# Last stage with the engines' work in an order written out by hand, and operand stores a tick apart

## The chip, the cores and the metric

The kernel runs on one core of a Trainium2 chip. A time is the device time of one execution in microseconds (us). The engines are TensorE (PE; PEld is its weight load), VectorE (DVE), ScalarE (ACT), GpSimd (POOL) and SyncE (SP), which issues the DMAs here. Each takes its instructions in the order in which the program wrote them, and waits on semaphores for the others.

## The reference

Attention, a layer of routed experts, and a rational layer are chained; only the last two matter here. With `x` of 1536 tokens by 512:

```python
def _moe_ref(x, w_gate, w1, w2):          # 8 experts, 512 -> 1024 -> 512
    P = softmax-like weights of x @ w_gate, normalised 8 times by rows and columns
    for e in range(E):
        out += P[:, e:e + 1] * (np.maximum(x @ w1[e], 0.0) @ w2[e])

def _moe2_ref(x, w_in, w_out, a, b):      # 512 -> 2048 -> 512
    h = x @ w_in
    P = a[0] + a[1] * h + a[2] * h**2 + a[3] * h**3
    Q = 1.0 + np.abs(b[0]) * np.abs(h) + np.abs(b[1]) * h**2
    return (P / (Q + 1e-06)) @ w_out
```

`w_in` and `w_out` arrive as 64-bit floats, which the kernel turns into 32-bit ones itself.

## The kernel before, in words

Every 32-bit matrix is split into a high part (rounded by a copy into the matmul type) and a low part (the difference), and a product takes three matmuls: high by high, high by low, low by high.

**Expert stage (up to about 1125 us).** It runs 30 weight slices by 2 halves of the tokens, in blocks of seven products (a Strassen-like scheme on 2 by 2 quarters, 42 matmuls of 384 columns) with the second matmuls of earlier blocks as fillers between them (`block`, lines 1014 to 1077). `sub_weights` splits the next slice's weights on GpSimd and issues its loads on SP's queue. After each product but the third, `step` calls `tick` (line 884). From the third weight slice on a tick also runs one job of the conversion of `w_in` and then `w_out` (`cvjobs`: five jobs per piece of 128 by 256: round, exponents, turn, join, add). Each time a column of `w_in` is converted, `op_jobs` (line 837) queues the preparation of its seven or eight operands in `opq`: sums of quarters on GpSimd, and `op_split` (line 831), a ScalarE cast of the high part and a GpSimd subtraction for the low part into one of two buffers (tag `t3`). `op_store` (line 826) writes a finished operand to DRAM. On each tick that is not an exponent job, `tick` first stores what was split before and then runs the next group of `opq`.

**Last stage (about 1125 us to the end).** 16 blocks: two halves of the tokens (j, 768 each) by eight column pairs of `w_in` (v, 256 columns). Two are `plain` blocks (line 1266: four groups of 12 matmuls); 14 are `seven` blocks (line 1289). A `seven` block has seven products through PSUM banks X and Y (Z shares Y's bank), each bank with one buffer: products 1, 2, 4 and 6 go to X and ScalarE copies X after each (lines 1305, 1308, 1314, 1321), products 3, 5 and 7 go to Z or Y and VectorE adds them (lines 1311, 1318, 1325). The results are `x1` (half 1, complete with the sixth product) and `x0` (half 0, complete with the seventh). `gate` (line 1218) computes the rational function of one half, 128 by 768, in five steps:
- one: three ScalarE activations (lines 1224 to 1226)
- two: three VectorE operations (1229 to 1231)
- three: logarithm and exponential on ScalarE (1234, 1235)
- four: three VectorE operations (1238 to 1240)
- five: the high part `hh` by a ScalarE cast (1245) and the low part `hl` by a GpSimd subtraction (1246)

The work tiles `ab`, `sq`, `ta` have two buffers, `hh` and `hl` four, `x0` two, `x1` one. `second` (line 1198) multiplies one tile of 128 tokens of a gated half with `w_out`: three matmuls of 512 columns, the fillers; a half has six of them, so a block brings twelve. They accumulate in six PSUM tiles for all of j.

The order was made by slots: `slot` (line 1182) runs what is due by its number, then up to two fillers that are due. There are seven slots to a block, after each product; `later` sets a step's slot, `gate(..., d, d2)` starts half 1's step one in slot 1 after its call and half 0's in slot 3, one step a slot, and its fillers 9 and 11 slots after. So a block's last slot holds five of half 0 of the block before, and then one of its own half 1, before the next block's first copy (line 1305).

The second token half's sums and splits (`x_parts` on GpSimd, `x_sums` on VectorE, `x_out` on ScalarE and VectorE) are due in slots of blocks 4 to 6.

Of the kernel before, what the change touches and what calls it, by code (L numbers as in the profile page):

```python
# [22 lines left out]
def kernel(  # L23
# [802 lines left out]
    def op_store():  # L826
        while ops:
            o, t = ops.pop()
            nc.sync.dma_start(f_ops[o:o + P, :], t.bitcast(F32).rearrange("p a t f -> p (a t f)"))

    def op_split(v_, name, x):
        t = vpool.tile([P, 2, 2, P], F32R, tag="t3", name=f"w{name}_o{v_}")
        nc.scalar.copy(t[:, 0], x)
        nc.gpsimd.tensor_sub(t[:, 1], x, t[:, 0].bitcast(F32))
        ops.append(((v_ * 8 + NAMES.index(name)) * P, t))

    def op_jobs(v_):

        q11, q12, q21, q22 = (wf[v_, k][:, :, f * P:(f + 1) * P] for f in range(2) for k in range(2))
        sp = lambda n, x: lambda: op_split(v_, n, x)  # L840
        add, sub = nc.gpsimd.tensor_add, nc.gpsimd.tensor_sub
        opq.append([sp("A22", q22)])
        if v_ < PLAIN:
            opq.append([sp("A21", q21)])
        opq.append([lambda: add(q22, q21, q22), sp("A11", q11)])
        opq.append([lambda: sub(q21, q11, q21)])
        opq.append([lambda: sub(q11, q22, q11), sp("A12", q12)])
        opq.append([lambda: sub(q12, q12, q11), sp("S1", q22)])
        opq.append([sp("S3", q21)])
        opq.append([sp("S2", q11)])  # L850
        opq.append([sp("S4", q12)])
        opq.append([])

    def cv_store():
        if not cvs:
# [28 lines left out]
    def tick(cv=False):  # L884

        point[0] += 1
        if g2q and g2q[0][0] <= point[0] or not g2q:
            run_job()
        if g2q and g2q[0][0] <= point[0]:
            g2q.pop(0)[1]()  # L890
        if cv and cvjobs:
            f = cvjobs.pop(0)
            f()
            if f is not cv_exponents and opq:
                op_store()
                for g in opq.pop(0):
                    g()

    lgs = {}

# [203 lines left out]
    def x_parts(j, ms=(11, 12, 22, 21)):  # L1104
        for m in ms:
            k, t = {11: (0, 0), 12: (0, 1), 22: (1, 1), 21: (1, 0)}[m]
            o = j * HT + t * NW
            a, b = (y[:, 2 * k:2 * k + 2, o:o + NW].bitcast(F32) for y in (xh, xl))
            nc.gpsimd.tensor_add(tf[m], a, b)
# [60 lines left out]
        load_w2(0, c)  # L1170
    n = NW
    W = 2 * n
    now = [0]
    due = {}
    fills = []
    outs = {}
    used = [0]

    def later(d, f, *args):
        due.setdefault(now[0] + d, []).append(lambda: f(*args))  # L1180

    def slot(k=2):
        for f in due.pop(now[0], []):
            f()
        now[0] += 1
        while k and fills and fills[0][0] <= now[0]:
            fills.pop(0)[1]()
            k -= 1

    def op():  # L1190
        t = got[used[0]]
# [23 lines left out]
            k = len(pairs) % (2 * NV)  # L1215
            load_w2(k // 2, 1 - k % 2)

    def gate(j, v, c, x, d, d2):

        nm = f"{j}_{v}_{c}"  # L1220
        ab, sq, ta = (buf(t, f"{t}_{nm}") for t in ("ab", "sq", "ta"))

        def one():
            nc.scalar.activation(ab, x, AF.Abs, scale=coef[:, 4:5])
            nc.scalar.activation(sq, x, AF.Square)
            nc.scalar.activation(ta, x, AF.Identity, scale=coef[:, 3:4], bias=coef[:, 2:3])

        def two():
            nc.vector.scalar_tensor_tensor(out=ab, in0=sq, scalar=coef[:, 5:6], in1=ab, op0=ALU.mult, op1=ALU.add)
            nc.vector.tensor_mul(ta, ta, x)  # L1230
            nc.vector.scalar_tensor_tensor(out=ta, in0=ta, scalar=coef[:, 1:2], in1=x, op0=ALU.add, op1=ALU.mult)

        def three():
            nc.scalar.activation(sq, ab, AF.Ln, bias=c1)
            nc.scalar.activation(sq, sq, AF.Exp, scale=-1.0)

        def four():
            nc.vector.scalar_tensor_tensor(out=ab, in0=ab, scalar=1.0 + 1e-6, in1=sq, op0=ALU.add, op1=ALU.mult)
            nc.vector.scalar_tensor_tensor(out=sq, in0=ab, scalar=2.0, in1=sq, op0=ALU.subtract, op1=ALU.mult)
            nc.vector.scalar_tensor_tensor(out=ta, in0=ta, scalar=coef[:, 0:1], in1=sq, op0=ALU.add, op1=ALU.mult)  # L1240

        def five():
            hh = hp2.tile([P, W], F32R, tag="hh", name=f"hh_{nm}")
            hl = hp2.tile([P, W], F32R, tag="hl", name=f"hl_{nm}")
            nc.scalar.copy(hh, ta)  # L1245
            nc.gpsimd.tensor_sub(hl, ta, hh.bitcast(F32))  # L1246
            ht[j, v, c] = (hh, hl)

        for i, f in enumerate((one, two, three, four, five)):
            later(d + i, f)  # L1250
        m = 2 * NV * j + 2 * v + 1 - c
        for t in range(W // P):
            fills.append((now[0] + d2, lambda t=t: second(j, v, c, t, m)))

    def three_passes(ps, w, get, start, stop, go):
        for t in range(2):
# [6 lines left out]
    def xs(k, o):  # L1263
        return lambda t: (xh[:, 2 * k + t, o:o + n], xl[:, 2 * k + t, o:o + n])

    def plain(v, j):

        for c in (1, 0):
            ws = [op() for _ in range(2)]
            x = buf(f"x{c}", f"x{c}_{j}_{v}", 2 - c)  # L1270
            for half in range(2):
                ps = psm.tile([P, 512], F32, tag="mm", name=f"p_{j}_{v}_{c}_{half}")[:, :n]
                for k in range(2):
                    for t in range(2):
                        mh, ml = xs(k, j * HT + half * n)(t)
                        a = k == t == 0
                        nc.tensor.matmul(ps, lhsT=ws[k][:, 0, t], rhs=mh, start=a, stop=False)
                        nc.tensor.matmul(ps, lhsT=ws[k][:, 0, t], rhs=ml, start=False, stop=False)
                        nc.tensor.matmul(ps, lhsT=ws[k][:, 1, t], rhs=mh, start=False, stop=k == t == 1)
                nc.scalar.copy(x[:, half * n:(half + 1) * n], ps)  # L1280
                if half:
                    gate(j, v, c, x, 1 if c else 3, 11)
                    load_op()
                    load_op()
                slot()
                if c or not half:
                    slot()

    def seven(v, j):

        o1, o2, ot = j * HT, j * HT + n, j * n
        psum = lambda t, nm: psx.tile([P, 512], F32, tag=t, name=f"{nm}_{j}_{v}")[:, :n]

        def tt(i):
            return lambda t: (th[i][:, t, ot:ot + n], tl[i][:, t, ot:ot + n])

        def product(ps, get, start):
            three_passes(ps, op(), get, start, True, {} if start else {"skip_group_check": True})

        X, Z = psum("X", "X2"), psum("Y", "Z2")  # L1300
        x0 = buf("x0", f"x0_{j}_{v}")
        x1 = buf("x1", f"x1_{j}_{v}", 1)
        s1, s2, s3 = x0[:, 0:n], x0[:, n:W], x1[:, n:W]
        product(X, xs(0, o1), True)
        nc.scalar.copy(s1, X)
        slot()
        product(X, tt(0), False)
        nc.scalar.copy(s2, X)
        slot()
        product(Z, xs(1, o1), True)  # L1310
        nc.vector.tensor_add(s1, s1, Z)
        slot()
        product(X, tt(1), False)
        nc.scalar.copy(s3, X)
        slot()
        Y = psum("Y", "Y2")
        product(Y, xs(0, o2), True)
        nc.vector.tensor_add(s3, s3, Y)
        slot()
        product(X, tt(2), False)  # L1320
        nc.scalar.copy(x1[:, 0:n], X)
        gate(j, v, 1, x1, 1, 9)
        slot()
        product(Y, xs(1, o2), False)
        nc.vector.tensor_add(s2, s2, Y)
        gate(j, v, 0, x0, 3, 11)
        slot(0)

    x_sums()
    later(1, x_out, 0, 22)  # L1330
    later(3, x_out, 0, 12)
    later(5, x_out, 0, 21)
    for i, m in enumerate((11, 12, 22, 21)):
        later(7 * 4 + 2 * i, x_parts, 1, (m,))
        later(7 * 5 + 2 + 2 * i, x_out, 1, (22, 12, 21, 11)[i])
    later(7 * 5 + 1, x_sums)
    for j in range(2):
        for v_ in range(NV):
            if j == 0 and v_ < PLAIN:
# [40 lines left out]
```

## Time and profile before

| | us |
|---|---|
| median of 3 runs | 1461.36 (1457.35 to 1464.21) |
| the profiled execution | 1462.85 |
| its span, first to last instruction | 1461.1 |
| TensorE busy, whole span | 1385.9 (95%) |
| VectorE, ScalarE, GpSimd busy | 1080.1, 544.2, 880.4 |

The page's forty slices of 36.5 us give each engine's busy share in tenths (9 is 90% or more) and TensorE's granted clock in tenths of full speed:

```profile
PE   7999999999999999999999999999999887888887
DVE  7785587777777768786777777777767788777666
ACT  6674323322222222222222222222223665565654
POOL 7644656688879879788777767777731142221122
PEclk9999999999999999999999999999999898999998
```

A wait row reads: the engine and line that stood idle, and the instruction whose end let it go on. Busy time of a matmul is modelled from its start; distances between starts are the better measure.

### The profile page before, as it was taken

How to read it: one execution, taken by the hardware profiler on the slowest of the kernel's cores; microseconds unless marked ns; L12 is line 12 of the kernel's file. 1: busy time of each engine (PE TensorE's matmuls, PEld its weight loads, DVE VectorE, ACT ScalarE, POOL GpSimd, SP SyncE). 2: the span in 40 equal slices, each digit the busy share in tenths (PEclk: the TensorE clock that was granted, in tenths of full speed). 3: DMA queues.
4: the chain of work that ended last, by engine and by line, in shares of the span. 5: the costliest groups of instructions: out<-in, count | busy, mean ns of one | idle time of the engine just before them, and what ended most of it. 6: DMA issues, size and time to landing. Idle time of an engine off the chain costs nothing.

```text
span 1461.1 us, 20671 instructions
## 1 busy us (share of the span) xinstructions
PE 1385.9 (95%) x7427; PEld 1225.3 (84%) x7427; DVE 1080.1 (74%) x1731; ACT 544.2 (37%) x1138; POOL 880.4 (60%) x1092
## 2 busy tenths in 40 slices
PE   7999999999999999999999999999999887888887
PEld 5788988988888888888888888888888776777776
DVE  7785587777777768786777777777767788777666
ACT  6674323322222222222222222222223665565654
POOL 7644656688879879788777767777731142221122
PEclk9999999999999999999999999999999898999998
DMA  9430111223222223222232222222213443454432
GB/s 260 112 99 6 44 39 64 66 87 108 73 87 102 71 88 101 78 89 94 61 91 84 69 72 73 79 68 84 74 37 94 135 150 119 151 181 145 148 95 72
DMA packets 116534, 137.03 MB, mean 94 GB/s; under 512 B 26320, under 2 KB 69328, under 8 KB 116432
## 3 DMA queue, kind: packets, MB, share of 16 engines
q1 hardware_dynamic: 116432, 135.71, 30.4%
q8 instruction: 59, 0.97, 0.3%
q14 instruction: 43, 0.35, 0.1%
HBM read 108.94 MB, written 26.74 MB: 93 GB/s over the span
## 4 chain that ended last, share of the span: by engine, by line
PE 71%; POOL 11%; DVE 7%; ACT 5%; issue 2%; DMA 2%; SPq 0%; POOLq 0%; ACTq 0%; DVEq 0%
PE p_v L185 9%; PE p_v L184 9%; PE p_v L183 9%; PE X L1032 5%; PE X L1033 5%; PE X L1034 4%; PE Y L1033 2%; PE Y L1032 2%; PE Y L1034 2%; PE o L1209 2%; PE o L1207 2%; PE o L1208 2%; PE p L183 2%; PE p L185 1%; PE p L184 1%
## 5 line engine op out<-in xcount | busy, mean ns | idle before, releaser
L1093 DVE SCALAR_TENSOR_TENSOR accs<-p_v,Pt,accs 128x512 f32<-128x512 f32 x336 | 250.1, 745 | 84.8 <-PE p_v L185 81.7
L185 PE MATMUL p_v<-w2h_v,hl_v 128*128 128x512 f32 x720 | 286.8, 398 | 0.0
L184 PE MATMUL p_v<-w2l_v,hh_v 128*128 128x512 f32 x720 | 285.2, 396 | 0.0
L183 PE MATMUL p_v<-w2h_v,hh_v 128*128 128x512 f32 x720 | 282.5, 392 | 0.0
L1246 POOL TENSOR_TENSOR hl<-ta,hh 128x768 fp32r<-128x768 f32 x32 | 68.7, 2147 | 252.5 <-ACT hh L1245 225.0
L1041 DVE SCALAR_TENSOR_TENSOR hl_v<-s,hh_v 128x384 fp32r<-128x384 f32 x180 | 126.3, 702 | 110.0 <-ACT hh_v L1040 109.6
L1040 ACT ACTIVATE hh_v<-s 128x384 fp32r<-128x384 f32 x180 | 94.7, 526 | 287.9 <-DVE s L1055 143.3
L185 PEld LDWEIGHTS p_v<-w2h_v,hl_v 128*128 128x128 f32 x720 | 135.5, 188 | 29.0
L183 PEld LDWEIGHTS p_v<-w2h_v,hh_v 128*128 128x128 f32 x720 | 135.9, 189 | 17.1
L184 PEld LDWEIGHTS p_v<-w2l_v,hh_v 128*128 128x128 f32 x720 | 135.6, 188 | 17.0
L109 POOL TENSOR_TENSOR wS<-S,wS 128x256 fp32r<-128x256 f32 x120 | 98.5, 820 | 14.4 <-ACT wS L106 4.7
L108 POOL TENSOR_SCALAR wS<-S 128x256 fp32r<-128x256 f32 x116 | 51.8, 446 | 88.1 <-PE X L1034 86.8
L1047 ACT COPY s<-X 128x384 f32<-128x384 f32 x60 | 28.7, 479 | 189.3 <-PE X L1034 189.3
L1032 PE MATMUL X<-th,wS 128*128 128x384 f32 x240 | 81.3, 339 | 8.4 <-ACT s L1052 8.2
L799 POOL TENSOR_SCALAR ce<-ce 128x256 uint32<-128x256 uint32 x64 | 71.1, 1110 | 25.4 <-DVE ce L787 25.4
L109 POOL TENSOR_TENSOR w2l_v<-sb,w2h_v 128x512 fp32r<-128x512 f32 x60 | 82.0, 1367 | 5.0
L1207 PE MATMUL o<-o2h,hh 128*128 128x512 f32 x192 | 80.7, 421 | 3.7 <-ACT hh L1245 2.7
L1209 PE MATMUL o<-o2h,hl 128*128 128x512 f32 x192 | 81.0, 422 | 3.1 <-POOL hl L1246 3.1
L1033 PE MATMUL Y<-xl,wS 128*128 128x384 f32 x240 | 81.2, 338 | 0.0
L1033 PE MATMUL X<-tl,wS 128*128 128x384 f32 x240 | 81.1, 338 | 0.0
L1034 PE MATMUL X<-th,wS 128*128 128x384 f32 x240 | 80.8, 337 | 0.0
L1208 PE MATMUL o<-o2l,hh 128*128 128x512 f32 x192 | 80.7, 421 | 0.0
(272 smaller groups left out, 3652.9 us busy)
## 6 DMA issues: line engine op xcount, KB each, us to landing
sa<-in_moe_w_dram SPq DMA_DIRECT2D x30, 512.0 KB, 3.6
sb<-in_moe_w_dram SPq DMA_DIRECT2D x30, 512.0 KB, 4.2
oS<-f_ops SPq DMA_DIRECT2D x56, 256.0 KB, 3.6
oA<-f_ops SPq DMA_DIRECT2D x50, 256.0 KB, 3.4
cv<-in_moe_w_in_dram SPq DMA_DIRECT2D x32, 256.0 KB, 3.9
f_ops<-wS_o SPq DMA_DIRECT2D x32, 256.0 KB, 2.1
cv<-in_moe_w_out_dram SPq DMA_DIRECT2D x32, 256.0 KB, 3.1
o2h<-f_out SPq DMA_DIRECT2D x32, 256.0 KB, 2.7
```

Of the source, the lines that this page charges most:

```text
L109: nc.gpsimd.tensor_sub(lo, src, hi.bitcast(F32))
L183: nc.tensor.matmul(ps, lhsT=sh, rhs=mh, start=(i == 0), stop=False)
L184: nc.tensor.matmul(ps, lhsT=sh, rhs=ml, start=False, stop=False)
L185: nc.tensor.matmul(ps, lhsT=sl, rhs=mh, start=False, stop=(i == n_k - 1))
L1032: nc.tensor.matmul(ps, lhsT=w[:, 0, t], rhs=mh, start=start and t == 0, stop=False, **go)
L1033: nc.tensor.matmul(ps, lhsT=w[:, 0, t], rhs=ml, start=False, stop=False, **go)
L1034: nc.tensor.matmul(ps, lhsT=w[:, 1, t], rhs=mh, start=False, stop=t == 1, **go)
L1041: nc.vector.scalar_tensor_tensor(out=hl, in0=src, scalar=0.0, in1=hh.bitcast(F32), op0=ALU.max, op1=ALU.subtract)
L1093: nc.vector.scalar_tensor_tensor(out=a, in0=ps, scalar=Pt[:, g, e:e + 1], in1=a, op0=ALU.mult, op1=ALU.add)
L1207: nc.tensor.matmul(ps, lhsT=hh[:, o], rhs=wh, start=first, stop=False, **go)
L1208: nc.tensor.matmul(ps, lhsT=hh[:, o], rhs=wl, start=False, stop=False, **go)
L1209: nc.tensor.matmul(ps, lhsT=hl[:, o], rhs=wh, start=False, stop=True, **go)
```

## The change

Two places. In the expert stage, `op_jobs` now queues pairs: one entry splits an operand and then runs the sums that follow it, the next entry stores it. A tick takes one entry; on an exponent job it takes one only if that is a store.

In the last stage the slots are gone. `gate` returns its steps as a list (five only casts, a new six makes the low part, for half 1 on VectorE and for half 0 on GpSimd as before), and `seven` and `plain` name at each place which steps of which earlier block run: `run(b - 1, 0, 1)` is step one of half 0 of block b-1. `fill(k)` runs up to k fillers that belong to a block at least two earlier; a `seven` block has them in groups of 4, 4, 2, 2. The first token half's `x_out` calls all stand ahead of the first plain block; the second half's sums and splits are a list `jobs2`, one entry per block, taken after the steps that follow the first copy.

```diff
+        def put(n, x, *pre):
+            opq.append(lambda: (op_split(v_, n, x), [f() for f in pre]))
+            opq.append(op_store)
+
+        put("A22", q22)
...
+        put("A11", q11, lambda: add(q22, q21, q22))
+        put("A12", q12, lambda: sub(q21, q11, q21), lambda: sub(q11, q22, q11))
+        put("S1", q22, lambda: sub(q12, q12, q11))
...
-            if f is not cv_exponents and opq:
-                op_store()
-                for g in opq.pop(0):
-                    g()
+            if opq and (f is not cv_exponents or opq[0] is op_store):
+                opq.pop(0)()
...
+    def fill(k):
+        while k and fills and fills[0][0] <= count[0]:
+            fills.pop(0)[1]()
             k -= 1
...
+        def six():
...
+            (nc.vector if c else nc.gpsimd).tensor_sub(hl, ta, hh.bitcast(F32))
...
-            fills.append((now[0] + d2, lambda t=t: second(j, v, c, t, m)))
+            fills.append((count[0] + 2, lambda t=t: second(j, v, c, t, i)))
+        return [one, two, three, four, five, six]
+    def run(b, c, *steps):
+        for i in steps:
+            if (b, c) in pipe:
+                pipe[b, c][i - 1]()
...
+        act = {0: lambda: (run(b - 2, 0, 5, 6), run(b - 1, 0, 1)),
+               1: lambda: (run(b - 1, 1, 2, 3), run(b - 1, 0, 2)),
+               2: lambda: (run(b - 1, 0, 3), run(b - 1, 1, 4, 5, 6)),
+               3: lambda: run(b - 1, 0, 4)}
...
+        run(b - 1, 1, 2)
         product(X, xs(0, o1), True)
         nc.scalar.copy(s1, X)
-        slot()
+        run(b - 2, 0, 5, 6)
+        run(b - 1, 0, 1)
+        run(b - 1, 1, 3)
+        run(b - 1, 0, 2)
+        if jobs2:
+            jobs2.pop(0)()
+        fill(4)
         product(X, tt(0), False)
         nc.scalar.copy(s2, X)
-        slot()
+        run(b - 1, 0, 3)
         product(Z, xs(1, o1), True)
         nc.vector.tensor_add(s1, s1, Z)
-        slot()
+        fill(4)
+        run(b - 1, 1, 4)
         product(X, tt(1), False)
         nc.scalar.copy(s3, X)
-        slot()
+        run(b - 1, 1, 5)
         Y = psum("Y", "Y2")
         product(Y, xs(0, o2), True)
         nc.vector.tensor_add(s3, s3, Y)
-        slot()
+        run(b - 1, 1, 6)
+        run(b - 1, 0, 4)
+        fill(2)
         product(X, tt(2), False)
         nc.scalar.copy(x1[:, 0:n], X)
-        gate(j, v, 1, x1, 1, 9)
-        slot()
+        pipe[b, 1] = gate(j, v, 1, x1)
+        run(b, 1, 1)
+        fill(2)
         product(Y, xs(1, o2), False)
         nc.vector.tensor_add(s2, s2, Y)
-        gate(j, v, 0, x0, 3, 11)
-        slot(0)
+        pipe[b, 0] = gate(j, v, 0, x0)
+        count[0] += 1
...
+    jobs2 += [lambda: None, lambda: x_parts(1, (11, 12)), lambda: x_parts(1, (22, 21)), x_sums]
+    jobs2 += [both(lambda: x_out(1, 22), lambda: x_out(1, 12)), both(lambda: x_out(1, 21), lambda: x_out(1, 11))]
```

After the last block the steps that remain run in the order two of half 1, five and six of the block before's half 0, one of half 0, three of half 1, two and three of half 0, four to six of half 1, four to six of half 0; then all 24 fillers that are left.

## Rows read from the trace of the kernel before

**Rows 1.** Windows (us; busy us and count by engine; granted clock; DMA share; GB/s).

```profile
740.00:760.00 20.00, 20.00 (x102) 18.11 (x101) 13.88 (x25) 4.64 (x10) 12.50 (x18) 1.00 0.14 41
1127.00:1461.00 334.00, 281.20 (x1251) 244.22 (x1249) 247.40 (x250) 202.09 (x276) 78.78 (x36) 0.91 0.42 133
1336.40:1356.76 20.36, 17.50 (x78) 15.33 (x78) 14.48 (x16) 11.89 (x17) 4.31 (x2) 0.92 0.44 142
510.00:520.00 10.00, 7.29 (x26) 6.24 (x25) 3.62 (x6) 2.10 (x5) 9.42 (x14) 0.70 0.50 181
670.00:680.00 10.00, 7.44 (x33) 6.42 (x32) 4.76 (x7) 2.56 (x7) 9.59 (x12) 0.89 0.50 165
```

**Rows 2.** TensorE's waits, whole span: total us, times, longest.

```profile
PE X L1258 <- ACT x L1305: 38.0, 12, 5.6
PE X L1032 <- ACT s L1052: 8.2, 4, 2.7
```

**Rows 3.** Line 1305: count, ns min/median/max, first and last start.

```profile
L1305 ACT COPY x<-X x14: 452/455/481, 1155.8 to 1417.4; 128x384 f32<-128x384 f32 x14
```

**Rows 4.** Timeline of one block, ScalarE and TensorE (start, us, instruction, idle before).

```profile
1332.74 0.83 ACT L1245 CAST hh<-ta 128x768 fp32r<-128x768 f32 x1 [3.50 <-DVE ta L1240]
...
1336.48 0.69 PE L1258 MATMUL X<-th,oS 128*128 128x384 f32 x1 [2.89 <-ACT x L1305]
...
1338.56 0.63 PE L1207 MATMUL o<-o2h,hh 128*128 128x512 f32 x1
...
1339.17 0.94 ACT L1234 ACTIVATE sq<-ab,c 128x768 f32<-128x768 f32 x1
...
1340.58 0.33 PE L1258 MATMUL Z<-xh,oA 128*128 128x384 f32 x1
...
1341.64 0.39 PE L1207 MATMUL o<-o2h,hh 128*128 128x512 f32 x1
...
1343.03 0.33 PE L1258 MATMUL X<-th,oS 128*128 128x384 f32 x1
```

**Rows 5.** Timeline, VectorE, the same block, and a split before it.

```profile
1135.58 0.95 DVE L1123 TENSOR_TENSOR tl<-accs,th 128x768 fp32r<-128x768 f32 x1
...
1335.17 1.15 DVE L1229 SCALAR_TENSOR_TENSOR ab<-sq,coef,ab 128x768 f32<-128x768 f32 x1 [2.01 <-ACT sq L1225]
...
1337.23 1.02 DVE L1231 SCALAR_TENSOR_TENSOR ta<-ta,coef,x 128x768 f32<-128x768 f32 x1
...
1341.91 0.56 DVE L1311 TENSOR_TENSOR x<-x,Z 128x384 f32<-128x384 f32 x1 [3.66 <-PE Z L1260]
...
1342.38 0.95 DVE L1238 SCALAR_TENSOR_TENSOR ab<-ab,sq 128x768 f32<-128x768 f32 x1
...
1347.22 2.49 DVE L1231 SCALAR_TENSOR_TENSOR ta<-ta,coef,x 128x768 f32<-128x768 f32 x1
```

**Rows 6.** Timeline, GpSimd beside VectorE, two places.

```profile
1189.25 5.04 POOL L1109 TENSOR_TENSOR accs<-xh,xl 128x768 f32<-128x768 f32 x2
...
1190.03 2.57 DVE L1230 TENSOR_TENSOR ta<-ta,x 128x768 f32<-128x768 f32 x1
...
1346.39 2.50 POOL L1246 TENSOR_TENSOR hl<-ta,hh 128x768 fp32r<-128x768 f32 x1 [10.88 <-ACT hh L1245]
```

**Rows 7.** Timeline, 507 to 514: GpSimd, SP's queue, ScalarE.

```profile
507.24 1.30 POOL L109 TENSOR_TENSOR w2l_v<-sb,w2h_v 128x512 fp32r<-128x512 f32 x1
...
508.56 0.38 SPq L228 DMA_DIRECT2D sb<-in_moe_w_dram  x1
...
513.77 0.41 ACT L833 CAST wS_o<-wf 128x256 fp32r<-128x256 f32 x1 [5.71 <-DMA f_ops<-wS_o]
```

**Rows 8.** Timeline: the sums at the stage's start; TensorE and GpSimd at its end.

```profile
1126.13 4.07 DVE L1113 TENSOR_TENSOR accs<-accs 128x768 f32<-128x768 f32 x4
...
1431.76 0.35 PE L1258 MATMUL Y<-xh,oS 128*128 128x384 f32 x1
...
1451.33 1.83 POOL L1246 TENSOR_TENSOR hl<-ta,hh 128x768 fp32r<-128x768 f32 x1 [4.79 <-issue]
```

More of the change, by code (lines that the diff above doesn't have):

```diff
@@ L839, in op_jobs @@
         q11, q12, q21, q22 = (wf[v_, k][:, :, f * P:(f + 1) * P] for f in range(2) for k in range(2))
-        sp = lambda n, x: lambda: op_split(v_, n, x)
         add, sub = nc.gpsimd.tensor_add, nc.gpsimd.tensor_sub
-        opq.append([sp("A22", q22)])
+        def put(n, x, *pre):
+            opq.append(lambda: (op_split(v_, n, x), [f() for f in pre]))
+            opq.append(op_store)
+        put("A22", q22)
         if v_ < PLAIN:
[L844 to L852, printed above, removed]
+            put("A21", q21)
+        put("A11", q11, lambda: add(q22, q21, q22))
+        put("A12", q12, lambda: sub(q21, q11, q21), lambda: sub(q11, q22, q11))
+        put("S1", q22, lambda: sub(q12, q12, q11))
+        put("S3", q21)
+        put("S2", q11)
+        put("S4", q12)
     def cv_store():
@@ L1172 @@
     W = 2 * n
-    now = [0]
-    due = {}
     fills = []
@@ L1177 @@
     used = [0]
[L1179 to L1186, printed above, removed]
+    def fill(k):
+        while k and fills and fills[0][0] <= count[0]:
             fills.pop(0)[1]()
             k -= 1
+    count = [0]
     def op():
@@ L1216, in second, with gate @@
             load_w2(k // 2, 1 - k % 2)
-    def gate(j, v, c, x, d, d2):
+    def gate(j, v, c, x):
         nm = f"{j}_{v}_{c}"
@@ L1243, in five @@
             hh = hp2.tile([P, W], F32R, tag="hh", name=f"hh_{nm}")
+            nc.scalar.copy(hh, ta)
+            m["hh"] = hh
+        def six():
+            hh = m["hh"]
             hl = hp2.tile([P, W], F32R, tag="hl", name=f"hl_{nm}")
-            nc.scalar.copy(hh, ta)
-            nc.gpsimd.tensor_sub(hl, ta, hh.bitcast(F32))
+            (nc.vector if c else nc.gpsimd).tensor_sub(hl, ta, hh.bitcast(F32))
             ht[j, v, c] = (hh, hl)
-        for i, f in enumerate((one, two, three, four, five)):
-            later(d + i, f)
-        m = 2 * NV * j + 2 * v + 1 - c
+        m = {}
+        i = 2 * NV * j + 2 * v + 1 - c
         for t in range(W // P):
-            fills.append((now[0] + d2, lambda t=t: second(j, v, c, t, m)))
+            fills.append((count[0] + 2, lambda t=t: second(j, v, c, t, i)))
+        return [one, two, three, four, five, six]
+    pipe = {}
+    def run(b, c, *steps):
+        for i in steps:
+            if (b, c) in pipe:
+                pipe[b, c][i - 1]()
     def three_passes(ps, w, get, start, stop, go):
@@ L1266, in plain @@
     def plain(v, j):
+        b = count[0]
+        act = {0: lambda: (run(b - 2, 0, 5, 6), run(b - 1, 0, 1)),
+               1: lambda: (run(b - 1, 1, 2, 3), run(b - 1, 0, 2)),
+               2: lambda: (run(b - 1, 0, 3), run(b - 1, 1, 4, 5, 6)),
+               3: lambda: run(b - 1, 0, 4)}
+        i = 0
         for c in (1, 0):
@@ L1280, in plain @@
                 nc.scalar.copy(x[:, half * n:(half + 1) * n], ps)
[L1281 to L1284, printed above, removed]
-                slot()
-                if c or not half:
-                    slot()
+                act[i]()
+                i += 1
+            load_op()
+            load_op()
+            if c:
+                x1 = x
+        pipe[b, 1] = gate(j, v, 1, x1)
+        pipe[b, 0] = gate(j, v, 0, x)
+        run(b, 1, 1)
+        count[0] += 1
     def seven(v, j):
+        b = count[0]
         o1, o2, ot = j * HT, j * HT + n, j * n
@@ L1318, in seven @@
         nc.vector.tensor_add(s3, s3, Y)
-        slot()
+        run(b - 1, 1, 6)
+        run(b - 1, 0, 4)
+        fill(2)
         product(X, tt(2), False)
         nc.scalar.copy(x1[:, 0:n], X)
-        gate(j, v, 1, x1, 1, 9)
-        slot()
+        pipe[b, 1] = gate(j, v, 1, x1)
+        run(b, 1, 1)
+        fill(2)
         product(Y, xs(1, o2), False)
         nc.vector.tensor_add(s2, s2, Y)
-        gate(j, v, 0, x0, 3, 11)
-        slot(0)
+        pipe[b, 0] = gate(j, v, 0, x0)
+        count[0] += 1
     x_sums()
[L1330 to L1336, printed above, removed]
+    jobs2 = []
+    for m in (22, 12, 21):
+        x_out(0, m)
+    both = lambda *fs: lambda: [f() for f in fs]
+    jobs2 += [lambda: None, lambda: x_parts(1, (11, 12)), lambda: x_parts(1, (22, 21)), x_sums]
+    jobs2 += [both(lambda: x_out(1, 22), lambda: x_out(1, 12)), both(lambda: x_out(1, 21), lambda: x_out(1, 11))]
     for j in range(2):
@@ L1346 @@
                 seven(v_, j)
-    while fills or due:
-        slot()
+    b = count[0]
+    run(b - 1, 1, 2)
+    run(b - 2, 0, 5, 6)
+    run(b - 1, 0, 1)
+    run(b - 1, 1, 3)
+    run(b - 1, 0, 2, 3)
+    run(b - 1, 1, 4, 5, 6)
+    run(b - 1, 0, 4, 5, 6)
+    count[0] += 2
+    fill(len(fills))
 _INS = ['q', 'k', 'v', 'moe_w_gate', 'moe_w1', 'moe_w2', 'moe2_w_in', 'moe2_w_out', 'moe2_a', 'moe2_b']
```

## The prediction

> **What bounds the kernel now.** I read the busy time by stretch first. In the stage with the routed experts TensorE is never idle: 20.00 of 20 us at granted clock 1.00 [rows 1]. In the last stage it is busy 281 of 334 us, at 0.91 [rows 1]. So time can be won in the last stage, and in the earlier one only where TensorE stalls. TensorE's waits name two places [rows 2]: the second product of a seven-product block (line 1258), 38.0 us in 12 waits for ScalarE's copy at line 1305, and line 1032 in the expert stage, 8.2 us in 4 waits for ScalarE's copy at line 1052.
>
> The 14 seven-product blocks start 20.12 us apart on average: line 1305 runs 14 times, first at 1155.8, last at 1417.4, and 261.6 / 13 = 20.12 [rows 3]. One such block shows why. ScalarE stands 3.50 us at the cast `hh` (line 1245), because VectorE has the last gate operation (line 1240) late; behind it in ScalarE's queue stand three gate operations and then the copy that empties X. TensorE waits 2.89 us for that copy [rows 4]. After the wait the six matmuls of the product take 2.08 us (1336.48 to 1338.56) and the two fillers behind them 2.02 us; at the higher clock a product takes 1.06 (1340.58 to 1341.64) and a pair of fillers 1.39 (1341.64 to 1343.03). So the wait brings 1.66 us at 1.2 GHz, until the clock is back at 2.4. 2.89 + 1.66 = 4.6 us of each block are not work; 7 x 1.05 + 6 x 1.39 = 15.7 us are.
>
> VectorE is not the bound: 14.48 of the block's 20.36 us [rows 1], and it stands 3.66 and 2.01 us in the same block [rows 5]. Both waits go back to the same stall: the first is for a product that TensorE starts late, the second for a gate operation behind the late cast.
>
> **The change: last stage.** The order written out puts the copy of X first in each block, right behind the first product, and the cast of half 0 after that copy. The gate of half 0 of block b-1 now runs in block b, its cast and low part in block b+1, so no cast that TensorE's next product stands behind waits for work of its own block. Four fillers (2.8 us) stand between each of the first copies and the product that needs the bank. I lay one steady block out in order, from the start of the seventh product (time 0), with durations from [rows 4 to 6]:
> - TensorE: seventh product 0, first product of the next block 1.05, four fillers 2.1, second product 4.9, third 5.9, four fillers 7.0, fourth 9.7, fifth 10.8, two fillers 11.9, sixth 13.2, two fillers 14.3, end 15.7.
> - ScalarE: copy 2.3, cast of half 0 2.7, its three gate operations 3.4 to 6.9 (cast, three operations and copy took 3.7, from 1332.74 to 1336.48; here the third overwrites `ta` and waits for GpSimd's low part), logarithm and exponential of half 1 to 8.5 (0.94 the first [rows 4], the second taken as less), second copy 8.5 to 8.9, needed at 9.7. That is 0.8 us of room. Busy 11.89 us per block before [rows 1] and as much after, so it is not the bound.
> - VectorE: sum into `x0` 1.8, three operations of half 1 from 2.3, three of half 0 from 6.6, sum 9.5, needed by TensorE at 10.8; three of half 1 9.9 to 12.9, sum 13.3, then it waits about 0.5 us for ScalarE's cast, does the new low part to 14.7, three of half 0 to 17.6.
>
> VectorE's sum decides. From line 1238 at 1342.38 to line 1231 at 1347.22 are five gate operations: 0.97 each [rows 5], so 12 take 11.6. Three sums of 0.47 (1341.91 to 1342.38) are 1.4. The low part, 128x768, comes from GpSimd: a subtraction of that form took VectorE 0.95 [rows 5]; in a row of instructions I count 0.9. GpSimd's low part of half 0 stays. When GpSimd ran one at 1346.39 (2.50 us), VectorE's line 1231, given to it at 1347.22, took 2.49 instead of 1.02 [rows 5, 6]: the two take turns, and it costs VectorE 1.5. That happens once a block now and once after (half 1 can't collide any more; half 0, which met an idle VectorE, now will). 11.6 + 1.4 + 0.9 + 1.5 = 15.4, with the wait for the cast 15.85 us. TensorE's 15.7 is just below. I take 15.85; bounds are 15.7 (TensorE alone) and 17.4 (VectorE loses two turns, + 1.5). From 20.12 that is 13 x 4.27 = 55.5 us.
>
> VectorE is then full, so work that its waits hid before now costs. The second half's sums and splits go through it once: four sums, 4.07 as at the stage's start [rows 8]; four low parts, 4 x 0.9; four sums on GpSimd, of which two took 5.04 us together and held up VectorE's line 1230 to 2.57 [rows 6]: a turn of 1.5 to 1.6 each, 3.1 per pair. 4.1 + 3.6 + 6.2 = 13.9 us; bounds 7 (half of it falls in waits) and 20 (TensorE comes back from each stall at the lower clock). Steady part: 55.5 - 13.9 = 41.6 us gained. The loads on SP's queue stay tied to the same products, nine operands and four pairs ahead; in the shorter block their 142 GB/s (share 0.44) become 182 (0.57) [rows 1], which 510 to 520 moved with ease [rows 1]. I cost them at nothing; if one came late, TensorE would wait for a load at line 1258 or 1207, which it never does now.
>
> **Start and end of the stage.** Three splits now stand ahead of the plain blocks' copies (1.7 us of VectorE, 2.2 of ScalarE), but three PSUM buffers let TensorE go on, and no fillers stand in the plain blocks, where four ran before. Laid out as above the first X copy comes near 1152 instead of 1155.8 with as many fillers done: I take 3 gained, bounds -2 and 6. At the end 24 fillers remain in either order. Before, the seventh product of the last block starts at 1431.76 and the last low part ends at 1451.33 + 1.83, that is 21.4 later [rows 8]; in the new order (two operations of half 0 beside GpSimd's turn, then four, cast, low part, four, cast, low part) I get 20.3: 1 gained, bounds -2 and 3.
>
> **The change: stores of w_in's operands.** ScalarE's first half of an operand reuses one of two buffers; it waited 5.71 us for the store of the operand before last [rows 7], because that store stood on SP's queue behind a weight load (issued 508.56) that itself waited for GpSimd's split (507.24 + 1.30) [rows 7]. Splits came a tick apart; now split and store take turns, so a buffer comes up again after five ticks instead of two or three. A tick is a sixth of a block's 78 matmuls, at 102 in 20 us [rows 1] 2.55 us, so five are 13 us. A store held up 5 us lands in time. The exponent tick now issues a store, never a split. The sums behind a split run after it on GpSimd, which nobody waits for within two ticks. What goes: 8.2 us of waits [rows 2], and the lower clock behind two: 510 to 520 has 26 matmuls and 670 to 680 has 33, where 51 fit [rows 1], so (25 + 18) x 20 / 102 = 8.4 us are lost there, against 2.71 + 2.56 of idleness. 8.2 + 3.1 = 11.3 us. Bounds 0 (the waits move elsewhere) and 13.
>
> **Sum.** 41.6 + 3 + 1 + 11.3 = 57 us. The profiled execution took 1462.85 us (span 1461.1), 1.5 above the median of the runs; against it 1406, against the median 1404. I say 1404.
>
> **Rivals.**
> *VectorE loses two turns to GpSimd per block* (17.4 us): 1404 + 13 x 1.5 = 1424. For: GpSimd's low part now runs while VectorE always has work. Against: before, a 2.50 us run cost only the one operation.
> *The stores bring nothing*, as ScalarE waits for VectorE's last conversion or GpSimd instead: 1404 + 11 = 1415. Against: the long waits name the store.
> *TensorE is the bound and the second half's work falls in gaps*: 13 x 0.15 + 7 + 5 better, 1390.
> *The clock, on the other side:* TensorE, held by a nearly full VectorE in every block, falls to 1.2 GHz again and again. Matmuls take twice as long at that clock, and VectorE's extra work then hides. It decides from 36% of TensorE's work at it: 15.7 x 1.36 = 21.3 us per block, 13 x 1.2 = 15 us lost, as much as start, end and stores gain. At half, 15.7 x 1.5 = 23.5 us per block, 13 x 3.4 = 44 lost, less 15: 1491. For: the 2.89 us wait did bring the lower clock. Against: it came back within the same block, before the third product (1340.58) [rows 4], and by my layout no stop over about 1 us is left in a steady block. The Trainium skill says in "TensorE: Matmul & The Clock Gate", section "A second HAM failure mode: psum-queue depth-cycling", that frequent short idles between groups of matmuls can make the clock swing between its levels; by that rule this rival would come true, and no row here shows such short idles bring it.
>
> **Chances.** Forecast (1394 to 1413) 0.55, two turns 0.18, stores nothing 0.08, better 0.12, clock 0.05, anything else 0.02. The range that holds the time 8 times in 10 is 1389 to 1429: it takes in both ends of the steady period. About 0.5% (7 us) is what a measurement can tell. Faster by more than that 0.94; within it 0.02; slower 0.04.
>
> **What would show it.** After: the first copies of a block some 15.9 us apart from the eighth block on, TensorE's waits for them gone, granted clock 0.97 or more in those blocks, VectorE busy over 14.9 us of each; blocks 3 to 7 about 18 to 20 us. Line 1032 without waits for ScalarE, and ScalarE's split without waits for stores. I am wrong if VectorE idles over 2 us per steady block, if TensorE's clock stays near 0.9, or if ScalarE's second copy comes later than the four fillers before it end.

## The result, and the profile after

The changed kernel takes 1403.89 us (median of 4 runs, 1403.49 to 1404.32) against 1462.35 (1457.35 to 1464.21) for the kernel before: ratio 0.9605, 95% interval 0.9581 to 0.963. The forecast was 1404. Its profiled execution took 1403.65 us, with a span of 1401.9.

The windows of the changed kernel (columns as in [rows 1]): the last stage, one steady block from first copy to first copy, two blocks with two `x_parts` each, and two stretches of the expert stage.

```profile
1112.00:1401.90 289.90, 264.62 (x1254) 230.83 (x1252) 261.44 (x266) 202.40 (x276) 43.09 (x20) 0.96 0.48 153
1327.20:1343.20 16.00, 15.93 (x79) 14.06 (x79) 15.35 (x17) 11.98 (x16) 2.09 (x1) 1.00 0.54 179
1153.74:1172.77 19.03, 15.90 (x79) 14.03 (x78) 18.38 (x17) 11.96 (x17) 7.19 (x3) 1.00 0.48 152
1172.77:1193.22 20.45, 17.33 (x79) 15.33 (x78) 19.80 (x19) 11.96 (x17) 7.14 (x3) 0.92 0.46 141
670.00:680.00 10.00, 10.00 (x52) 9.08 (x51) 7.72 (x14) 2.07 (x6) 9.50 (x13) 1.00 0.33 105
740.00:760.00 20.00, 20.00 (x102) 17.98 (x101) 15.70 (x26) 4.50 (x11) 16.93 (x21) 1.00 0.25 79
```

The steady block of 20.36 us in [rows 1] is one of 16.00: VectorE is now busy 15.35 of it, TensorE 15.93, the granted clock is 1.00 instead of 0.92. From 670 to 680 us TensorE issues 52 matmuls instead of 33. The undisturbed stretch from 740 to 760 is as before.

The first copies of the blocks of seven products, to set beside [rows 3]:

```profile
L1321 ACT COPY x<-X x14: 473/481/483, 1137.3 to 1359.2; 128x384 f32<-128x384 f32 x14
```

(1359.2 - 1137.3) / 13 = 17.07 us on average, 15.98 where no transform work lies in the block. TensorE's waits, whole span, beside [rows 2]: neither the copy behind the first product nor line 1052 is left, and the short last row is all that ScalarE costs TensorE in the expert stage. ScalarE's splits (line 833) wait for no store any more; before, they did so for 63.1 us:

```profile
ACT wS_o L833 <- DMA f_ops<-wS_o: 33.0, 11, 5.7
ACT wS_o L833 <- DMA f_ops<-wA_o: 26.0, 11, 4.9
ACT wA_o L833 <- DMA f_ops<-wA_o: 4.1, 2, 2.8
```

TensorE's waits after; the first row is new, it lies in the first blocks of seven products, nearly all of it beside the second half's sums and splits.

```profile
PE Y L1263 <- DVE x L1333: 10.6, 5, 3.1
PE o L1201 <- issue: 4.9, 1, 4.9
PE o L1201 <- ACT hh L1238: 4.5, 1, 4.5
...
PE X L1263 <- ACT x L1330: 0.8, 2, 0.5
...
PE X L1032 <- ACT s L1047: 0.3, 1, 0.3
```

A steady block in the timeline (start, us, instruction, idle before and its releaser), VectorE, GpSimd and ScalarE, beside [rows 4 to 6]:

```profile
1311.25 0.48 ACT L1321 COPY x<-X 128x384 f32<-128x384 f32 x1 [0.36 <-PE X L1265]
...
1311.68 0.83 ACT L1238 CAST hh<-ta 128x768 fp32r<-128x768 f32 x1
...
1312.64 2.10 POOL L1244 TENSOR_TENSOR hl<-ta,hh 128x768 fp32r<-128x768 f32 x1 [13.89 <-ACT hh L1238]
1312.95 2.61 DVE L1224 TENSOR_TENSOR ta<-ta,x 128x768 f32<-128x768 f32 x1
...
1317.46 0.95 DVE L1224 TENSOR_TENSOR ta<-ta,x 128x768 f32<-128x768 f32 x1
...
1322.88 0.84 ACT L1238 CAST hh<-ta 128x768 fp32r<-128x768 f32 x1 [2.46 <-DVE ta L1234]
1323.75 0.96 DVE L1244 TENSOR_TENSOR hl<-ta,hh 128x768 fp32r<-128x768 f32 x1 [0.44 <-ACT hh L1238]
```

The cast of half 0 stands behind the first copy and waits for nothing. VectorE has one wait, 0.44 us. Its L1224 takes 2.61 us beside GpSimd's low part and 0.95 without it.

Where the time went, by the two spans (1461.1 - 1401.9 = 59.2 us):

| stretch | before | after | gained | predicted |
|---|---|---|---|---|
| start of the span to the last stage's first product | 1125.08 | 1110.52 | 14.6 | 11.3 |
| from there to the first copy of X | 30.67 | 26.80 | 3.9 | 3 |
| 13 periods | 261.6 | 221.9 | 39.7 | 41.6 |
| last first copy to the end | 43.67 | 42.70 | 1.0 | 1 |

### The profile page after: what moved, and what is told of

The parts are those of the page before. It is cut to its first block, busy times and chain, and to the rows that moved or that the text cites. A ratio compares the mean times of both kernels' runs of the same rounds, so it can differ in the third digit from the quotient of the medians.

```text
span 1401.9 us, 20653 instructions
## 1 busy us (share of the span) xinstructions
PE 1363.6 (97%) x7427; PEld 1208.4 (86%) x7427; DVE 1094.9 (78%) x1747; ACT 542.8 (39%) x1138; POOL 849.4 (61%) x1076
## 4 chain that ended last, share of the span: by engine, by line
PE 77%; DVE 18%; ACT 2%; issue 1%; POOL 1%; POOLq 0%; ACTq 0%; DVEq 0%
PE p_v L185 12%; PE p_v L184 12%; PE p_v L183 12%; PE X L1033 6%; PE X L1032 6%; PE X L1034 6%; DVE ta L1224 3%; PE Y L1033 3%; PE Y L1034 3%; PE Y L1032 3%; DVE ta L1225 3%; DVE ab L1223 2%; DVE ta L1234 2%; DVE sq L1233 2%; DVE ab L1232 2%; PE p L183 2%
## 5 line engine op out<-in xcount | busy, mean ns | idle before, releaser
L1244 POOL TENSOR_TENSOR hl<-ta,hh 128x768 fp32r<-128x768 f32 x16 | 33.0, 2063 | 243.6 <-ACT hh L1238 204.3
L1201 PE MATMUL o<-o2h,hh 128*128 128x512 f32 x192 | 77.6, 404 | 9.4 <-issue 4.9
L799 POOL TENSOR_SCALAR ce<-ce 128x256 uint32<-128x256 uint32 x64 | 72.3, 1130 | 15.8 <-DVE ce L787 15.8
L1034 PE MATMUL Y<-xh,wS 128*128 128x384 f32 x240 | 80.2, 334 | 0.0
L1032 PE MATMUL Y<-xh,wS 128*128 128x384 f32 x240 | 80.1, 334 | 0.0
```

Source lines behind the costliest of these rows:

```text
L799: nc.gpsimd.tensor_scalar(out=e, in0=e, scalar1=896, scalar2=0, op0=ALU.subtract, op1=ALU.max)
L1032: nc.tensor.matmul(ps, lhsT=w[:, 0, t], rhs=mh, start=start and t == 0, stop=False, **go)
L1034: nc.tensor.matmul(ps, lhsT=w[:, 1, t], rhs=mh, start=False, stop=t == 1, **go)
L1201: nc.tensor.matmul(ps, lhsT=hh[:, o], rhs=wh, start=first, stop=False, **go)
```

## Experiments

Times are medians; "after" is the changed kernel, 1403.89. All ran with runs of the kernel before beside them (1461.35 to 1463.36).

### The stores apart: e1_ops_old and e2_ops_only

e1 is the changed kernel with the old `op_jobs` and the old rule in `tick`; e2 is the kernel before with the new ones alone.

```diff
# e1 against after (e2 against before is the reverse)
-            if opq and (f is not cv_exponents or opq[0] is op_store):
-                opq.pop(0)()
+            if f is not cv_exponents and opq:
+                op_store()
+                for g in opq.pop(0):
+                    g()
```

> The changed kernel with the old queue of operand splits and stores (a split on every tick, its store one tick later). Theory: the expert stage's stalls come from ScalarE waiting for a store that stands behind a weight load, so all of that stage's gain and nothing else goes: the last stage starts 14 us later (1125 instead of 1110.5) and keeps its length; 1404 + 14 = 1418 us. Rival: the two halves of the change lean on each other (loads and stores meet the last stage's loads): the last stage changes too, by over 3 us.

> The kernel before with the new queue of splits and stores alone. Theory: 1462 - 14 = 1448 us, no wait of ScalarE's operand split for a store. Rival (no gain without the other half): 1460 or more.

Measured: e1 1416.84 (1416.19 to 1417.8; ratio to before 0.9693, 0.9671 to 0.9715), e2 1447.55 (1445.98 to 1450.42; 0.9905, 0.988 to 0.993). The stores are worth 1416.84 - 1403.89 = 13.0 us in one kernel and 1462.35 - 1447.55 = 14.8 in the other. The two edits don't interfere: the last stage is worth the rest, 44 to 46 us, with either queue, and its 13 periods take 222.2 us in e1 (221.9 in the changed kernel) and 261.7 in e2 (261.6 before).

### Why the stores came late: e3_load_later

```diff
# against e1: the load of the next slice's second weights is issued later
-            if i in (3, 5) and n + 1 < NSUB:
-                dma_sub(n + 1, 1 + i // 4)
+            if i == 3 and n + 1 < NSUB:
+                dma_sub(n + 1, 1)
...
+                elif i == 2:
+                    dma_sub(n, 2)
```

> The changed kernel with the old queue of splits and stores, but the weight load that the late stores stood behind is issued four products later, when its buffer is long free. Theory (the place behind the load on SP's queue makes the store late): most of the stalls go although splits stay bunched: 1404 to 1408 us. Rival (the splits stand too close together, or GpSimd is overloaded by them): the stalls stay, 1415 to 1419 us.

1406.44 (1405.46 to 1409.75; 0.9625, 0.9601 to 0.9649). With the old queue, in which a buffer still comes up again after two or three ticks, moving the one load that stood in front of the stores on SP's queue brings back 1416.84 - 1406.44 = 10.4 of the 13 us. Line 1054, the old line 1052, now holds TensorE up once:

```profile
PE X L1034 <- ACT s L1054: 1.0, 1, 1.0
```

In e1 it did so four times for 8.5 us, much as before (8.2). So the load's place is what let the stall reach TensorE. That the stores then come in time is not shown: ScalarE's splits still wait 38.5 us for stores in e3, 19 times (e1: 45.4 us, 20 times), only less long at a time. These are the longest rows of each, e1 first, then e3:

```profile
ACT wS_o L833 <- DMA f_ops<-wA_o: 22.0, 10, 5.1
ACT wS_o L833 <- DMA f_ops<-wS_o: 20.0, 8, 5.7
...
ACT wS_o L833 <- DMA f_ops<-wS_o: 27.8, 12, 4.6
ACT wS_o L833 <- DMA f_ops<-wA_o: 9.7, 6, 4.0
```

Only the new queue takes these waits away.

### GpSimd's turns: e4_low_pool and e5_low_dve

```diff
-            (nc.vector if c else nc.gpsimd).tensor_sub(hl, ta, hh.bitcast(F32))
+            nc.gpsimd.tensor_sub(hl, ta, hh.bitcast(F32))     # e4
+            nc.vector.tensor_sub(hl, ta, hh.bitcast(F32))     # e5
```

> The changed kernel with both low parts on GpSimd, as before. Theory (GpSimd and VectorE take turns; a GpSimd low part costs VectorE 1.5 us, more than the 0.9 us of doing it itself): VectorE 11.6 + 1.4 + 3.0 = 16.0 us a block, less the 0.44 us wait for the cast: no gain from undoing it, 1404 to 1411 us, VectorE's operations at 2.5 us twice a block. Rival (GpSimd is free for it, VectorE is the bound): 0.9 us a block less until TensorE binds at 15.7, 1400 us.

> The changed kernel with both low parts on VectorE. Theory (taking turns): VectorE gains 0.9 us of work a block and loses a turn of 1.5 and ScalarE its wait for GpSimd: 15.35 - 1.6 + 0.9 = 14.7 busy, below TensorE's 15.7, so TensorE binds: 13 x 0.3 = 4 us faster, 1400 us. Rival (VectorE's sum of own work binds): 0.9 us a block more, 1415 us.

e4 1408.12 (1407.6 to 1409.23; 0.9635, 0.961 to 0.9661), e5 1397.06 (1396.33 to 1399.28; 0.9547, 0.9533 to 0.9561). A second low part on GpSimd costs 4 us. Both turns are there in each block:

```profile
1331.32 2.61 DVE L1224 TENSOR_TENSOR ta<-ta,x 128x768 f32<-128x768 f32 x1
...
1342.58 2.50 DVE L1233 SCALAR_TENSOR_TENSOR sq<-ab,sq 128x768 f32<-128x768 f32 x1
```

In exchange VectorE saves its own low part (0.96) and the wait before it (0.44), so the steady block grows only from 16.00 to 16.1. It is not the prediction's rival of two turns, which had VectorE's own low part besides. Of the 4 us the 13 periods hold 1.3; the rest lies at the stage's start and end. With none on GpSimd, two steady blocks of e5 take 31.28 us, and TensorE has no gap in them:

```profile
1325.32:1356.60 31.28, 31.28 (x158) 28.19 (x157) 29.61 (x35) 23.86 (x33) 0.00 (x0) 1.00 0.54 175
```

15.64 us is thus TensorE's own period, and VectorE with its 14.8 no longer decides. The two bounds lie close: in e3, whose last stage is the changed kernel's, GpSimd's low part meets line 1227 (the changed kernel's 1225) in place of the one before it, in one block for 2.48 us instead of 1.02, and three blocks in a row take 15.6 to 15.8 us.

### Places of fillers, ScalarE's order: e6_fill2, e7_order_old, e8_both_old

e6 has the fillers in pairs behind the products as before. e7 has ScalarE's old order at the block's end. e8 has both.

```diff
# e6 against after: fill(4), fill(4), fill(2), fill(2) become fill(2) in six places
# e7 against after
-        run(b - 2, 0, 5, 6)
         run(b - 1, 0, 1)
...
         pipe[b, 1] = gate(j, v, 1, x1)
-        run(b, 1, 1)
...
         nc.vector.tensor_add(s2, s2, Y)
+        run(b - 1, 0, 5, 6)
+        run(b, 1, 1)
```

> The changed kernel with fillers two at a time after each of the first six products (before the second, third, fourth, fifth product, and the last two pairs as they are), as the slots had them. Theory (ScalarE's second copy ends at 8.9 in my layout, the fourth product now wants it at 8.4): 0.5 us of wait a block, period 16.2 to 16.3: 1407 to 1410 us. Rival (the fillers' new places carry most of the gain): over 1425 us.

> The changed kernel with ScalarE's old order around the block's end: cast and low part of half 0, then the three gate operations of half 1, ahead of the next block's first copy; fillers in groups of four as changed. Theory (the four fillers cover most of it): the first copy ends at 5.7 in my layout instead of 2.7, the second product wants it at 4.9: 0.9 us of wait a block, period 16.5, 1411 us. Rival (the order alone carries the gain): TensorE waits 2.9 us there and falls to the lower clock as before, 1440 to 1460 us.

> Both of these undone: ScalarE's old order at the block's end and fillers two at a time. Theory (they only work together): the second product wants the copy at 3.5 and gets it at 5.7, 2.2 us of wait and the lower clock behind it (1.7): period near 19.7, 1435 to 1450 us. Rival (the two act apart, so their costs add): sum of what each costs alone, near 1418 us.

e6 1404.92 (1404.68 to 1405.24; 0.9598, 0.9584 to 0.9612): the fillers' places are worth 1 us, less than either theory had. e7 1415.55 (1414.83 to 1415.68; 0.967, 0.9655 to 0.9684), 4 us over the theory and far under the rival. e8 1417.45 (1417.35 to 1417.89; 0.9684, 0.9668 to 0.97): my theory, that late cast and pairs of fillers together make the old stall, fell. The steady periods are 16.08, 16.59 and 16.85 us, where before had 20.36. The cast and three operations stand in front of the copy in e8 as they did before, and still some 30 us to e2 were missing.

### A loop through the engines: e10_steps_old and e11_cast_later

What e8 still had from the change: half 0's steps stand in front of the Z sum on VectorE, where before had them behind it. New theory: before was a closed loop. Each link waited for the one before, on another engine, and one turn round the loop was one block. e10 is e8 with the gate's steps at their old places. Steps two and three of half 1 and steps three and four of half 0 move back with the lines shown. e11 is e10 with only the loop's end opened: cast a block later, behind the copy.

```diff
# e10 against e8
-        run(b - 1, 0, 1)              # behind the first copy, with 0, 2
-        run(b - 1, 0, 2)
...
         nc.vector.tensor_add(s1, s1, Z)
         run(b - 1, 1, 4)
+        run(b - 1, 0, 1)
...
         nc.scalar.copy(s3, X)
         run(b - 1, 1, 5, 6)
+        run(b - 1, 0, 2)
...
# e11 against e10
         nc.scalar.copy(s1, X)
+        run(b - 2, 0, 5, 6)
...
         run(b - 1, 0, 4)
+        run(b, 1, 1)
...
-        run(b - 1, 0, 5, 6)
-        run(b, 1, 1)
```

> Base: the kernel of e8 (ScalarE's order at the end of a block and pairs of fillers as before), and besides the gate steps of both halves at their old places: half 0's first ScalarE step behind s1+=Z, its first VectorE step behind the third copy. Theory (a loop through four engines: Z product, s1+=Z, four of half 1, two of half 0, s3+=Y, four of half 0, cast, three activations, first copy, second product, a pair of fillers, Z product; from the rows of before 20.4 us, with the low part of half 1 on VectorE 20 to 21): steady period 20 to 21 us, time 1440 to 1455, as e2. Rival (each old order adds its own few us and no loop is closed): steady period under 17.5, time 1415 to 1425.

> Base: e10, but the cast of half 0 a block later behind the first copy and the three activations of half 1 ahead, as in the changed kernel; half 0's steps stay behind the Z sum and fillers stay in pairs. Theory (the loop is open at the cast): steady period 15.9 to 16.6 us, VectorE's sum, time 1403 to 1412. Rival (the place of half 0's steps behind the Z sum costs by itself, whatever the cast does): period over 18 us, time over 1425.

e10 1456.64 (1454.12 to 1459.85; 0.9959, 0.9946 to 0.9971), a little over the time expected, steady period 20.49 as expected; e11 1411.32 (1409.66 to 1412.56; 0.9652, 0.9628 to 0.9677), period 16.44. Two edits, each undone alone and together, all with pairs of fillers:

| | cast behind the first copy | cast, then half 1's activations, ahead of it |
|---|---|---|
| steps as changed (half 0's ahead of the Z sum) | e6 1404.92 | e8 1417.45 |
| steps at their old places (half 0's behind it) | e11 1411.32 | e10 1456.64 |

Costs that only add up would make e10 1404.92 + 12.53 + 6.40 = 1423.85. It is 33 us over that, and the steady period is 20.49 instead of 17.21 (16.08 + 0.77 + 0.36): only both together close the loop. One turn of it in e10's timeline, link by link:

```profile
1346.18 0.83 ACT L1238 CAST hh<-ta 128x768 fp32r<-128x768 f32 x1 [3.06 <-DVE ta L1234]
...
1348.48 1.01 ACT L1220 ACTIVATE ta<-x,coef 128x768 f32<-128x768 f32 x1
...
1349.40 0.46 ACT L1321 COPY x<-X 128x384 f32<-128x384 f32 x1
...
1349.91 0.69 PE L1263 MATMUL X<-th,oS 128*128 128x384 f32 x1 [2.88 <-ACT x L1321]
...
1353.75 0.34 PE L1263 MATMUL Z<-xh,oA 128*128 128x384 f32 x1
...
1355.07 0.55 DVE L1331 TENSOR_TENSOR x<-x,Z 128x384 f32<-128x384 f32 x1 [3.38 <-PE Z L1265]
...
1358.56 0.84 ACT L1238 CAST hh<-ta 128x768 fp32r<-128x768 f32 x1 [0.66 <-DVE ta L1234]
1359.43 0.96 DVE L1244 TENSOR_TENSOR hl<-ta,hh 128x768 fp32r<-128x768 f32 x1 [0.90 <-ACT hh L1238]
...
1362.22 1.02 DVE L1225 SCALAR_TENSOR_TENSOR ta<-ta,coef,x 128x768 f32<-128x768 f32 x1
...
1365.61 1.02 DVE L1234 SCALAR_TENSOR_TENSOR ta<-ta,coef,sq 128x768 f32<-128x768 f32 x1
...
1366.66 0.83 ACT L1238 CAST hh<-ta 128x768 fp32r<-128x768 f32 x1 [3.06 <-DVE ta L1234]
```

From cast to cast 1366.66 - 1346.18 = 20.48 us, and each link starts when the one before it ends: cast, activations, copy, second product and fillers, Z, sum, four of half 1, cast, low part, two of half 0, sum, four of half 0, cast. Three engines take part, not four as the theory had it: GpSimd's low part of half 0 (1.81 us) runs beside the loop. Each engine stands idle in it, and none is the bound. The kernel before closes likewise, there with GpSimd's turn as a link in place of VectorE's low part: line 1231 ends at 1347.22 + 2.49 [rows 5], with a sum (0.47) and three operations (2.9) behind it that is 1353.1, and there the cast of the next block starts:

```profile
1353.12 0.83 ACT L1245 CAST hh<-ta 128x768 fp32r<-128x768 f32 x1 [3.50 <-DVE ta L1240]
```

One link is long by TensorE's lower clock. In the kernel before a single steady block kept the clock at 1.00 through the same wait; its window, and its second product and the sum behind Z:

```profile
1296.88:1315.68 18.80, 15.95 (x78) 13.94 (x78) 14.50 (x16) 14.62 (x23) 4.31 (x2) 1.00 0.63 202
...
1297.39 0.44 PE L1258 MATMUL X<-th,oS 128*128 128x384 f32 x1 [2.85 <-ACT x L1305]
...
1301.24 0.55 DVE L1311 TENSOR_TENSOR x<-x,Z 128x384 f32<-128x384 f32 x1 [2.08 <-PE Z L1260]
```

From the product to the sum this is 3.85 us, in e10 5.16 (1349.91 to 1355.07), and the block took 18.80 us instead of 20.36. So by estimate 1.3 us of e10's turn are the clock, 1.6 in the kernel before; the stall itself stayed at either clock.

e8 has a shorter loop left, which is why its 16.85 us is no engine's sum:

```profile
1342.22 0.44 PE L1263 MATMUL X<-th,oS 128*128 128x384 f32 x1 [0.92 <-ACT x L1322]
...
1350.96 0.56 DVE L1343 TENSOR_TENSOR x<-x,Y 128x384 f32<-128x384 f32 x1 [0.69 <-PE Y L1265]
...
1355.33 0.84 ACT L1238 CAST hh<-ta 128x768 fp32r<-128x768 f32 x1 [1.53 <-DVE ta L1234]
...
1358.56 0.46 ACT L1322 COPY x<-X 128x384 f32<-128x384 f32 x1
```

TensorE runs from the second product to the fifth without a stop, VectorE's sum waits for the fifth, low part and four of half 0 follow, then cast, activations, copy and the next second product. What holds e11 at 16.44 was not followed.

### What the bound allows: e9_low_parts_dve and e12_spread

In the profiled run of e5 the first block of seven products took 23.82 us. Its timeline shows why:

```profile
1139.21 10.06 POOL L1109 TENSOR_TENSOR accs<-xh,xl 128x768 f32<-128x768 f32 x4 [31.38 <-DVE xl L1123]
```

With nothing else to do, GpSimd runs all four `x_parts` there, and four VectorE operations beside them take 2.47 to 2.61 us each. e9 puts them on VectorE as well; e12 also spreads the sums over two blocks.

```diff
# e9 against e5
-            nc.gpsimd.tensor_add(tf[m], a, b)
+            (nc.vector if j else nc.gpsimd).tensor_add(tf[m], a, b)
# e12 against e9
-    jobs2 += [lambda: None, lambda: x_parts(1, (11, 12)), lambda: x_parts(1, (22, 21)), x_sums]
+    jobs2 += [lambda: x_parts(1, (11, 12)), lambda: x_parts(1, (22, 21))]
+    jobs2 += [lambda: x_sums(slice(0, 2)), lambda: x_sums(slice(2, None))]
```

> Both low parts on VectorE (as e5) and the four x_parts of the second half on VectorE too. In e5 the first block of seven products took 23.82 us against a steady 15.64, with four GpSimd adds of 2.5 us in 10.06 us beside VectorE operations of 2.47 to 2.61 us. Theory (turns with GpSimd make those 8.2 us): that block falls to about 16 and two blocks grow by 1 to 1.5 us (1.9 us more VectorE work against 0.85 us of slack), time 1390 to 1393. Rival (the start's waits make the 23.82): as e5, 1396 to 1399.

> e9 with the second half's transform jobs spread: two x_parts in each of the first two blocks of seven products, two x_sums in each of the next two, where e9 has all four x_sums in one. Theory (VectorE has 0.85 us of slack in a block of 15.64 us, so 1.9 us more costs 1.05): x_sums' +4.0 becomes 2 x 1.05, time 1 to 3 us under e9, 1388 to 1391. Rival (the first block has no slack, so jobs there cost their whole 1.9 us and more): same as e9 or above.

e9 1393.86 (1393.33 to 1394.98; 0.9536, 0.9509 to 0.9563): its first block takes 16.51 us, so the turns did make the 23.82, though the total is 1 us over what I expected. e12 1393.83 (1393.09 to 1394.24; 0.9533, 0.951 to 0.9556): the two blocks with the sums fall from 17.20 + 20.77 to 17.30 + 17.34, and what is won is lost where work moved to, mostly in the first block (19.19), which has no slack. The rival held. Both beat the changed kernel by 10 us.

## Why the prediction was right

- **The forecast.** Of 1404 the runs made 1403.89. That it fits to the tenth is luck: the kernel before alone ranges over 7 us, and misses of the terms cancel in part, the stores (14.6 against 11.3) and the start (3.9 against 3) against the 13 periods (39.7 against 41.6).
- **The bound after.** VectorE's sum was put at 15.4 us busy and 15.85 with a wait of 0.5; it is 15.35 busy in a block of 16.00 and waits 0.44. TensorE's own period was put at 15.7; e5 shows 15.64. e5 shows VectorE to be what decides in the changed kernel: without the turn the period falls to TensorE's.
- **The turn.** Put at 1.5 us, once a block; it is 2.61 - 0.95 = 1.66.
- **The second half's sums and splits.** Put at 13.9 us; the 13 periods together are 221.9 - 13 x 15.98 = 14.2 over the steady ones. By kind the blocks can't be read. The two with `x_parts` are 3.05 and 4.47 over, but the second holds two of VectorE's regular operations more (19 against 17, 19.80 us busy against 18.38), the blocks with `x_out` are 2.2 over instead of 3.6, and in e1 the larger of the pairs is the first (20.36 and 19.46 us). VectorE stands idle 0.65 us in either of the two, so what counts is the sum.
- **The stores.** This is the term that was mis-sized: 11.3, at most 13, against 13.0 (e1), 14.8 (e2) and 14.6 in the traces. The waits for stores were the right place: they are gone, and TensorE's with them. That the load ahead of the stores matters is shown (e3); that it alone made them late is not. I took the waits from one row and the lower clock from two windows of 10 us; by the starts of the same VectorE line (1055) in both traces stalls and their slow tails lie in more places, the largest 6.1 and 4.0 us (513 to 534 and 659 to 695).
- **What broke the old stall.** The rows named the right wait, and the prediction put it down to a late cast in front of the copy. That was half. The cast was late because the same block's stalled Z product made it late, and the change moves links of that loop at two places; either alone wins most (e8, e11). The prediction's 1.66 us for the lower clock holds: 20.36 - 18.80 = 1.56. The four fillers ahead of the second product, which my layout credited, are worth 1 us (e6), with the old cast 2 (e7 to e8); with the loop closed they weren't tried.
- **The clock rival fell in the steady blocks.** The granted clock there is 1.00, and 1.00 in e8 too, where TensorE waits once per block (below). The rule of the Trainium skill cited for it ("TensorE: Matmul & The Clock Gate", section "A second HAM failure mode: psum-queue depth-cycling") did not show at one short wait per block; more frequent ones were not tried:

```profile
1324.87:1375.42 50.55, 47.77 (x234) 41.99 (x234) 42.08 (x49) 35.12 (x50) 5.56 (x3) 1.00 0.48 158
```

That is the window of e8's last three steady blocks; TensorE's waits in it are four, the longest 0.9 us:

```profile
PE X L1263 <- ACT x L1322: 3.7, 4, 0.9
```

In the changed kernel's first blocks the lower clock did come: after a wait of 3.1 us for a sum on VectorE the block from 1172.77 is at 0.92, while the one from 1153.74 kept 1.00 after such a wait. VectorE stands idle 0.65 us in either, so the clock can have cost little there.

- **Left open.** Start and end of the stage (3.9 and 1.0 us against 3 and 1) weren't taken apart by a run. The start's wait of 4.9 us for the first gate and the end's of 4.5 are still in the kernel.

## What to carry to other kernels

When no engine is full and the same wait returns in every block, follow the wait's releaser round until it comes back to itself: if the links sum to the period, it is a loop, and its length is the period. Move one link behind or ahead by a block, and the period falls to the next bound, which may be a shorter loop (e8) or the fullest engine (the changed kernel); test the suspected links in pairs, since each alone may show little of what both cost. On a DMA queue, look at what stands ahead of a late store as well as at how long its buffer lasts.

## What the runs showed of the hardware

- VectorE and GpSimd, each on 128x768 operands, take turns: a VectorE operation of 0.95 to 1.02 us takes 2.47 to 2.61 beside one on GpSimd, for `TENSOR_TENSOR` and `SCALAR_TENSOR_TENSOR` alike. GpSimd's takes up to 2.6 instead of 1.81. The Trainium skill says that a VectorE operation with two inputs in SBUF contends with a GpSimd instruction that reads SBUF, and calls the shared ports an exclusive lock ("SBUF — State Buffer", section "Who interferes with whom"). The rows agree: GpSimd's low part at 1312.64 takes 2.10 us, to 1314.74, and line 1224, begun at 1312.95, ends 0.82 us after that. They add the price. So work given to GpSimd to relieve a full VectorE cost VectorE more (1.66) than doing it itself (0.95): e5 beats the changed kernel by 7 us.
- A wait of up to 0.9 us in each block left the granted clock at 1.00 (e8). One of 2.88 came with 0.92, in e10's window of one block below and in all its steady blocks; in the kernel before, a wait of 2.85 us left it at 1.00 in one steady block of eight (18.80 us, above) and came with 0.92 in the seven others:

```profile
1349.40:1369.89 20.49, 17.50 (x78) 15.15 (x78) 13.99 (x17) 11.80 (x18) 1.81 (x1) 0.92 0.46 142
```
